# Score buffers of two PSUM banks for a pair of heads, and a fixed order of a pair's products and masks

## The chip, the core and the metric

One program runs on one core of a Trainium2 chip. The metric is the device time of one execution in microseconds (us); of several executions the median is taken. Five engines work side by side: TensorE (PE; PEld is its weight load), VectorE (DVE), ScalarE (ACT), GpSimd (POOL) and SyncE (SP, which here only issues DMAs). TensorE writes its results to PSUM, eight banks of 128 partitions by 512 floats.

## The reference

Block-causal attention (blocks of 64) over 4 batches, 8 heads, 576 positions and 64 channels; then a mixture of 8 experts on the 2304 tokens whose gates are normalised eight times by rows and columns; then a soft mixture of 8 experts with 32 slots.

```python
scores = scale * np.matmul(q, k.transpose(0, 1, 3, 2))
scores = np.where(mask, scores, -1000000000.0)
scores = scores - np.max(scores, axis=-1, keepdims=True)
attn = np.exp(scores)
attn = attn / (np.sum(attn, axis=-1, keepdims=True) + 1e-09)
return np.matmul(attn, v).astype(np.float32)
...
for e in range(E):
    h = np.maximum(x @ w1[e], 0.0)
    ye = h @ w2[e]
    out += P[:, e:e + 1] * ye
```

## The kernel before

Only the attention stage is touched, the first 340 us or so. It works on pairs of heads: 4 batches of 4 pairs. The 576 queries of a head are cut into four tiles of 128 (j = 0 to 3) and a last one of 64; the two heads' last ones share a tile (a = 2, j = 4). A tile of number j needs 128(j+1) keys, so its score product is 128, 256, 384 or 512 columns wide. The list `jobs` has four jobs with j = 0 and 1 only (four steps each, for the first batch, so that the mixture of experts can begin early), four with j = 2, 3 and 4 (five steps) and twelve with all (nine steps). A step is one tile of one head; head 0 and head 1 alternate.

One step `g` of the loop at L598 emits in this order: the scores (`emit_S`; at head 0 for both heads), the row maximum on DVE (`emit_max`), the transposes of the step four before (`emit_T`, on PE, with a copy out of PSUM on ACT, L488), the exponential on ACT (`emit_exp`, L451, with a read of its accumulator), the scaling by the reciprocal sum (`emit_scale`, L457 and L458 on DVE, L471 on POOL), then what `todo` holds: value products (`emit_PV`, L527) and the split of their result into a high and a low part (L545, L549). Then `fill` asks a generator (`moe_stream`) for mixture-of-experts (MoE) matmuls worth a nominal 1200 ns: first layer L174 to L176, second layer L203. It gives none while the batch that it needs next is not through attention.

A planner puts the instructions of each engine into a fixed order ahead of time: by program order among those that are ready in its own forecast, with a tile's slot allocated when one is free. `tc.keep_in_program_order(x)` adds one condition: x comes behind the instruction that was traced just before it on its engine; it doesn't forbid others in between. On the chip each engine takes its instructions in that order and waits on semaphores.

The PSUM banks in the attention stage: two (`m0`, `m1`) for the MoE work and, in the first four jobs, for the transposes; one (`pv`) for the value products; five (`tag="s"`, `SB = 5`) that scores of head 0, scores of head 1 and later transposes take one by one, as they come free. The scores of a pair: two products with 64 rows each (each is two matmul instructions, since it is in float32), head 0 on partitions 0 to 63, head 1 on 64 to 127, in separate banks; then two small bfloat16 products that add the mask. The two halves of TensorE's rows can run at the same time. The last tile (L420 to L426) has eight matmuls into two banks; its transposes (L502 to L509) take two banks, `tp` and `tq`. The probability tiles `pes` (j < 2) and `pe` have three buffers each; a transposed tile frees one.

Loads of MoE weights go through one raw buffer (`r`); L120 (ACT) and L121 (DVE or POOL) split them into a high and a low part, the pieces of the second layer pinned in program order.

Of the kernel before, what the change touches and what calls it, by code (L numbers as in the profile page):

```python
# [7 lines left out]
F32 = mybir.dt.float32  # L8
# [26 lines left out]
def attn_moe_softmoe_kernel(ctx: ExitStack, tc: tile.TileContext, qk1, q, k, v, wg, w1, w2, phi, m2w1, m2w2, cst, out):  # L35
    nc = tc.nc
# [28 lines left out]
    def bank(name):  # L65
        pool, tag = banks[nbank[0] % len(banks)]
        nbank[0] += 1
        return pool.tile([128, 512], F32, tag=tag, name=name)
# [281 lines left out]
    with ExitStack() as actx:  # L350
        ap1 = actx.enter_context(tc.tile_pool(name="at1", bufs=1))
        ap2 = actx.enter_context(tc.tile_pool(name="at2", bufs=2))
        ps = actx.enter_context(tc.tile_pool(name="ps", bufs=1, space=PSUM))

        mask_l = ap1.tile([128, 128], BF16, name="mask_l")
        mask_r = ap1.tile([128, 64], BF16, name="mask_r")
# [5 lines left out]
        def tiles_of(gr):  # L362
            return (G1 if "1" in gr else []) + (G2 if "2" in gr else [])
# [31 lines left out]
            x = qk[n][0][:, 256:S + 64] if gr == "2" else qk[n][0]  # L395
            nc.gpsimd.tensor_scalar(out=x, in0=x, scalar1=0.125, scalar2=1.0, op0=ALU.mult, op1=ALU.mult)

        SB = 5
        EPOOL = False
        PS_ = 3  # L400
        PB_ = 3
# [2 lines left out]
        HD = [slice(0, 64), slice(64, 128)]  # L404

        def emit_S(n, tl):
            a, j = tl
            qt, kt = qk[n]
            if a == 1:
                return st_S[n, j]  # L410
            if a == 0:
                w = 128 * (j + 1)
                ss = [ps.tile([128, 512], F32, tag="s", name="s", bufs=SB) for _ in range(2)]
                for r, s in zip(HD, ss):
                    nc.tensor.matmul(s[:, 0:w], qt[r, 128 * j:128 * j + 128], kt[r, 0, 0:w], start=True, stop=False)  # L415
                for r, s in zip(HD, ss):
                    nc.tensor.matmul(s[:, 128 * j + 64:128 * j + 128], mask_l[r], mask_r[r], start=False, stop=True)
                st_S[n, j] = [ss[1][:, 0:w]]
                return [ss[0][:, 0:w]]
            sv = [ps.tile([128, 512], F32, tag="s", name="sL", bufs=SB)[:, 0:288] for _ in range(2)]  # L420
            for x in range(2):
                for hf in range(2):
                    r = HD[hf]
                    h = hf ^ x
                    nc.tensor.matmul(sv[hf][HD[h]], qt[r, 512 + 64 * x:576 + 64 * x], kt[r, x, 288 * hf:288 * hf + 288], start=True, stop=True)  # L425
            return sv  # L426
# [49 lines left out]
        def emit_T(n, t, pt):  # L476
            p, gr = jobs[n]
            a, j = tiles_of(gr)[t]
            if (a, j) == (0, 0):
                PT[n, 0] = ap1.tile([128, 2, 384], F32, tag="PT0", name="PT0")  # L480
            if (a, j) == (0, 2):
                PT[n, 1] = (ap1.tile([128, 2, 4, 320], F32, tag="PT1", name="PT1"), ap1.tile([64, 2, 64], F32, tag="PT2", name="PT2"))

            def cp(o, i):
                if n < 4 and a == 1:
                    nc.vector.tensor_copy(out=o, in_=i)
                else:
                    nc.scalar.activation(out=o, in_=i, func=AF.Copy)  # L488
            if j < 4:
                if nofill[0]:  # L490
                    tp = bank("tp")
                else:
                    tp = ps.tile([128, 512], F32, tag="s", name="tp", bufs=SB)
                for i in range(j + 1):
                    nc.tensor.transpose(tp[:, 128 * i:128 * i + 128], pt[:, 128 * i:128 * i + 128], ident)  # L495
                if j < 2:
                    cp(PT[n, 0][:, a, 128 * j:128 * j + 128 * (j + 1)], tp[:, 0:128 * (j + 1)])
                else:
                    cp(PT[n, 1][0][:, a, 0:j + 1, 128 * (j - 2):128 * (j - 2) + 128], tp[:, 0:128 * (j + 1)].rearrange("p (i q) -> p i q", q=128))
                return  # L500
            big, small = PT[n, 1]
            tp = ps.tile([128, 512], F32, tag="s", name="tp", bufs=SB)  # L502
            for i in range(4):
                nc.tensor.transpose(tp[:, 128 * i:128 * i + 128], pt[:, 128 * i:128 * i + 128], ident)
            tq = ps.tile([128, 512], F32, tag="s", name="tq", bufs=SB)
            nc.tensor.transpose(tq[0:64, 0:128], pt[:, 512:576], ident)
            for a in range(2):
                cp(big[:, a, :, 256:320], tp.rearrange("p (i a q) -> p a i q", a=2, q=64)[:, a])
            cp(small, tq[0:64, 0:128].rearrange("p (a q) -> p a q", a=2))  # L509
# [88 lines left out]
        for g in range(NG + LT + 6):  # L598
            live = g < NG
            if live:  # L600
                n, t = steps[g]
                p, gr = jobs[n]
                ntl = len(tiles_of(gr))
                tl = tiles_of(gr)[t]
                sv = emit_S(n, tl)
                nm = emit_max(sv)
            fill(FILL * FR)
            if 0 <= g - LT < NG:
                emit_T(*steps[g - LT], st[g - LT][0])
# [46 lines left out]
    tq = [tmp[j // 2][:, H_ * (j % 2):H_ * (j % 2) + H_] for j in range(4)]  # L656
# [245 lines left out]
    for u in range(4, NU - 1):  # L902
        i = ND + u - 4
# [444 lines left out]
```

## Time and profile before

| | before |
|---|---|
| median of 3 runs | 1810.55 us (1809.51 to 1810.71) |
| profiled execution | 1809.36 us |
| its span, first to last instruction | 1807.6 us |
| granted TensorE clock, mean | 0.998 |
| PE, DVE, ACT, POOL busy | 98%, 66%, 32%, 12% of the span |

The page's slices are 45 us each; the attention stage is the first seven and a half. A timeline row merges neighbours of the same kind: start, time from the first one's start to the last one's end, engine, line, operation, what is written and read, shape and count, and in brackets the idle time before it with what ended it. Matmuls overlap, so the distance between two starts says more than a duration.

### The profile page before, as it was taken

The numbers are of one execution on the slowest core, as the hardware profiler recorded it, in microseconds if no ns is written. First come the engines' busy times: TensorE is split into PE (matmuls) and PEld (weight loads), VectorE is DVE, ScalarE is ACT, GpSimd is POOL, SyncE is SP. The second block draws the span as 40 slices with busy tenths as digits, with TensorE's granted clock in tenths as the row PEclk, the third lists the DMA queues.
The fourth block names the chain that finished last, engine by engine and source line by source line (L and its number), as shares of the span: only waits on it lengthen the run. The fifth ranks groups of instructions, "written<-read, shape, count | busy, mean of one in ns | idle before, by whom it ended". The sixth has DMA issues, their size and how long they took to land.

```text
span 1807.6 us, 24545 instructions
## 1 busy us (share of the span) xinstructions
PE 1779.8 (98%) x9239; PEld 1411.1 (78%) x9239; DVE 1197.5 (66%) x2391; ACT 584.7 (32%) x1485; POOL 225.4 (12%) x343
## 2 busy tenths in 40 slices
PE   7999999999999999999999999999999999999997
PEld 4676666787888888888888888888888888888864
DVE  5566555688766676677776666667777766666542
ACT  5666656334322222222222222222222222222232
POOL 4333222033000000000000000000000000000011
PEclk9999999999999999999999999999999999999999
DMA  5432311011000000000000000000000000000877
GB/s 178 128 101 82 101 55 61 13 48 36 24 24 24 24 24 24 24 24 24 17 19 24 24 24 24 24 24 24 24 24 24 24 24 24 24 24 16 298 278 274
DMA packets 79046, 102.98 MB, mean 57 GB/s; under 512 B 4688, under 2 KB 55632, under 8 KB 78928
## 3 DMA queue, kind: packets, MB, share of 16 engines
q1 hardware_dynamic: 78928, 101.42, 16.9%
q8 instruction: 73, 1.20, 0.3%
q14 instruction: 45, 0.37, 0.1%
HBM read 96.68 MB, written 4.72 MB: 56 GB/s over the span
## 4 chain that ended last, share of the span: by engine, by line
PE 91%; DVE 2%; POOL 1%; ACT 1%; issue 1%; DMA 1%; ACTq 0%; POOLq 0%; SPq 0%; DVEq 0%
PE l L203 42%; PE S L804 17%; PE A L804 12%; PE pvp L527 2%; PE tp L495 2%; PE s L415 2%; PE l L854 2%; PE l L853 2%; PE l L852 2%; PE l L174 1%; PE l L176 1%; PE l L175 1%; DMA r<-in_moe_w_dram 1%; PE xt L944 1%; PE sL L425 0%
## 5 line engine op out<-in xcount | busy, mean ns | idle before, releaser
L213 DVE SCALAR_TENSOR_TENSOR acc<-l,P,acc 128x512 f32<-128x512 f32 x504 | 377.9, 750 | 224.3 <-PE l L203 223.8
L203 PE MATMUL l<-w2h,hh 128*128 128x512 f32 x1132 | 447.9, 396 | 1.0 <-ACT hh L807 1.0
L203 PE MATMUL l<-w2h,hl 128*128 128x512 f32 x1132 | 443.0, 391 | 1.3 <-DVE hl L808 1.1
L203 PE MATMUL l<-w2l,hh 128*128 128x512 f32 x1132 | 442.8, 391 | 0.0
L819 DVE TENSOR_TENSOR tmp<-S,tmp 128x512 f32<-128x512 f32 x275 | 185.0, 689 | 138.1 <-PE S L804 136.4
L203 PEld LDWEIGHTS l<-w2h,hl 128*128 128x128 f32 x1132 | 212.9, 188 | 47.7 <-DVE hl L808 1.7
L203 PEld LDWEIGHTS l<-w2h,hh 128*128 128x128 f32 x1132 | 213.2, 188 | 46.1 <-ACT hh L807 1.5
L203 PEld LDWEIGHTS l<-w2l,hh 128*128 128x128 f32 x1132 | 213.3, 188 | 39.9
L807 ACT ACTIVATE hh<-tmp 128x512 fp32r<-128x512 f32 x216 | 136.1, 630 | 290.6 <-DVE tmp L819 261.0
L804 PE MATMUL S<-T,es 128*128 128x512 f32 x660 | 167.3, 389 | 0.0
L778 POOL TENSOR_TENSOR st<-r 128x256 f32<-128x256 f32 x56 | 41.0, 753 | 987.3 <-DMA r<-in_moe_w_dram 987.3
L804 PE MATMUL A<-xh,es 128*128 128x512 f32 x440 | 153.4, 389 | 0.0
L804 PE MATMUL S<-xh,es 128*128 128x512 f32 x440 | 153.4, 389 | 0.0
L808 DVE SCALAR_TENSOR_TENSOR hl<-tmp,hh 128x512 fp32r<-128x512 f32 x216 | 147.9, 685 | 0.8 <-ACT hh L807 0.7
L804 PEld LDWEIGHTS S<-T,es 128*128 128x128 f32 x660 | 123.9, 188 | 25.7
L661 ACT ACTIVATE es<-st 128x256 fp32r<-128x256 f32 x112 | 46.5, 415 | 211.2 <-POOL st L778 112.7
L823 ACT ACTIVATE tmp<-A 128x512 f32<-128x512 f32 x55 | 32.8, 597 | 234.9 <-PE A L804 233.3
L120 ACT ACTIVATE w2h<-r 128x256 fp32r<-128x256 f32 x160 | 54.5, 407 | 144.0 <-PE l L203 126.1
L804 PEld LDWEIGHTS S<-xh,es 128*128 128x128 f32 x440 | 82.6, 188 | 17.1
L804 PEld LDWEIGHTS A<-xh,es 128*128 128x128 f32 x440 | 82.6, 188 | 17.1
L819 DVE TENSOR_TENSOR tmp<-A,tmp 128x512 f32<-128x512 f32 x110 | 75.7, 688 | 16.9 <-PE A L804 16.3
L804 PE MATMUL A<-xl,es 128*128 128x512 f32 x220 | 85.7, 389 | 0.0
(231 smaller groups left out, 2538.5 us busy)
## 6 DMA issues: line engine op xcount, KB each, us to landing
r<-in_moe_w_dram SPq DMA_DIRECT2D x80, 512.0 KB, 3.4
mw<-in_moe_w_dram SPq DMA_DIRECT2D x64, 512.0 KB, 7.4
kraw<-in_k_dram SPq DMA_DIRECT2D x16, 576.0 KB, 3.9
qraw<-in_q_dram SPq DMA_DIRECT2D x16, 320.0 KB, 4.3
v<-in_v_dram SPq DMA_DIRECT2D x16, 256.0 KB, 2.9
out_dram<-ob SPq DMA_DIRECT2D x6, 512.0 KB, 3.5
out_dram<-ob SPq DMA_DIRECT2D x6, 256.0 KB, 2.3
qk<-in_qk_dram SPq DMA_DIRECT2D x4, 256.0 KB, 4.4
```

The lines of the kernel that those rows point to most:

```text
L120: p = [nc.scalar.activation(out=h, in_=r[:, a:a + 256], func=AF.Copy)]
L203: nc.tensor.matmul(o, lh, w[:, kf, :], start=(m == 0), stop=(m == 5))
L213: nc.vector.scalar_tensor_tensor(out=av, in0=o, scalar=P[:, tt, e:e + 1], in1=av, op0=ALU.mult, op1=ALU.add)
L415: nc.tensor.matmul(s[:, 0:w], qt[r, 128 * j:128 * j + 128], kt[r, 0, 0:w], start=True, stop=False)
L495: nc.tensor.transpose(tp[:, 128 * i:128 * i + 128], pt[:, 128 * i:128 * i + 128], ident)
L527: nc.tensor.matmul(o[64 * a:64 * a + 64, lo:hi], w, r(a), start=(m == 0), stop=(m == len(its) - 1))
L661: nc.scalar.activation(out=h, in_=src, func=AF.Copy),
L778: nc.gpsimd.tensor_tensor(out=o, in0=a, in1=b, op=alu)
L804: nc.tensor.matmul(o[:, 0:H_], a[:, k], b[:, k], start=(k == 0 and m == 0), stop=(k == 1 and m == 2))
L807: nc.scalar.activation(out=h, in_=src, func=AF.Relu)
L808: nc.vector.scalar_tensor_tensor(out=lo, in0=src, scalar=0.0, in1=f32(h), op0=ALU.max, op1=ALU.subtract)
L819: nc.vector.tensor_tensor(out=out, in0=o, in1=i, op=ALU.add)
```

## The change

Scores of both heads share one tile of two banks (`s2`), with two such buffers in place of the five single banks; the last tile's scores and the last tile's transposes (`t2`) use the same two buffers; the other transposes get one bank of their own (`tag="tp"`). The second head's product is pinned behind the first head's, and each mask behind what was traced before it. The number of instructions does not change.

```diff
-        SB = 5
...
             if a == 0:
                 w = 128 * (j + 1)
-                ss = [ps.tile([128, 512], F32, tag="s", name="s", bufs=SB) for _ in range(2)]
+                s2 = ps.tile([128, 2, 512], F32, tag="s", name="s", bufs=2)
+                ss = [s2[:, 0], s2[:, 1]]
                 for r, s in zip(HD, ss):
-                    nc.tensor.matmul(s[:, 0:w], qt[r, 128 * j:128 * j + 128], kt[r, 0, 0:w], start=True, stop=False)
+                    i = nc.tensor.matmul(s[:, 0:w], qt[r, 128 * j:128 * j + 128], kt[r, 0, 0:w], start=True, stop=False)
+                    if r is HD[1]:
+                        tc.keep_in_program_order(i)
                 for r, s in zip(HD, ss):
-                    nc.tensor.matmul(s[:, 128 * j + 64:128 * j + 128], mask_l[r], mask_r[r], start=False, stop=True)
+                    tc.keep_in_program_order(nc.tensor.matmul(s[:, 128 * j + 64:128 * j + 128], mask_l[r], mask_r[r], start=False, stop=True))
                 st_S[n, j] = [ss[1][:, 0:w]]
                 return [ss[0][:, 0:w]]
-            sv = [ps.tile([128, 512], F32, tag="s", name="sL", bufs=SB)[:, 0:288] for _ in range(2)]
+            s2 = ps.tile([128, 2, 512], F32, tag="s", name="sL", bufs=2)
+            sv = [s2[:, 0, 0:288], s2[:, 1, 0:288]]
...
                 if nofill[0]:
                     tp = bank("tp")
                 else:
-                    tp = ps.tile([128, 512], F32, tag="s", name="tp", bufs=SB)
+                    tp = ps.tile([128, 512], F32, tag="tp", name="tp")
...
-            tp = ps.tile([128, 512], F32, tag="s", name="tp", bufs=SB)
+            t2 = ps.tile([128, 2, 512], F32, tag="s", name="tp2", bufs=2)
+            tp, tq = t2[:, 0], t2[:, 1]
             for i in range(4):
                 nc.tensor.transpose(tp[:, 128 * i:128 * i + 128], pt[:, 128 * i:128 * i + 128], ident)
-            tq = ps.tile([128, 512], F32, tag="s", name="tq", bufs=SB)
             nc.tensor.transpose(tq[0:64, 0:128], pt[:, 512:576], ident)
```

## Rows read from the trace of the kernel before

**Rows 1.** The page: busy time (us, share, instructions) and shares of the last chain.
```profile
PE 1779.8 (98%) x9239; PEld 1411.1 (78%) x9239; DVE 1197.5 (66%) x2391; ACT 584.7 (32%) x1485; POOL 225.4 (12%) x343
...
PE 91%; DVE 2%; POOL 1%; ACT 1%; issue 1%; DMA 1%; ACTq 0%; POOLq 0%; SPq 0%; DVEq 0%
```

**Rows 2.** Timeline of PE, 195 to 210 us, a nine-step job with fill.
```profile
202.79 0.70 PE L415 MATMUL s<-kraw,qraw 64*128 64x256 f32 x4
...
207.37 0.92 PE L415 MATMUL s<-kraw,qraw 64*128 64x384 f32 x4
...
208.51 2.42 PE L527 MATMUL pvp<-PT,v 128*64 128x320 f32 x20
```

**Rows 3.** Timeline of PE, 225.9 to 228 us, a pair that comes apart.
```profile
225.99 0.70 PE L415 MATMUL s<-kraw,qraw 64*128 64x256 f32 x2
226.62 0.50 PE L203 MATMUL l<-w2h,hl 128*128 128x512 f32 x1
...
227.71 0.66 PE L495 MATMUL tp<-ident,pe 128*128 128x128 f32 x4
```

**Rows 4.** Timeline of PE at 184.8 us, masks that stand apart.
```profile
184.83 0.20 PE L417 MATMUL s<-mask_r,mask_l 64*128 64x64 bf16 x2
```

**Rows 5.** Timeline of PE, 147 to 157 us, a crowded pass.
```profile
147.34 0.63 PE L495 MATMUL tp<-ident,pe 128*128 128x128 f32 x4
147.89 0.91 PE L415 MATMUL s<-kraw,qraw 64*128 64x256 f32 x4
...
149.72 0.48 PE L203 MATMUL l<-w2h,hl 128*128 128x512 f32 x1
150.13 1.19 PE L415 MATMUL s<-kraw,qraw 64*128 64x384 f32 x4
...
151.28 0.33 PE L495 MATMUL tp<-ident,pes 128*128 128x128 f32 x1
...
155.83 1.03 PE L425 MATMUL sL<-kraw,qraw 64*64 64x288 f32 x8
```

**Rows 6.** Timeline of ACT, 147 to 152 us, the same pass.
```profile
147.57 0.49 ACT L488 ACTIVATE PT<-tp 128x384 f32<-128x384 f32 x1
...
150.78 0.27 ACT L488 ACTIVATE PT<-tq 64x128 f32<-64x128 f32 x1
151.65 0.47 ACT L451 ACTIVATE pes<-s,nm 128x256 f32<-128x256 f32 x1 [0.60 <-PE tp L495]
```

**Rows 7.** Timeline of PE, 4 to 21 us, the start.
```profile
4.47 1.21 PE L415 MATMUL s<-qk 64*128 64x256 f32 x4
...
6.59 1.47 PE L415 MATMUL s<-qk 64*128 64x256 f32 x4
...
16.27 1.22 PE L415 MATMUL s<-qk 64*128 64x256 f32 x2
...
19.71 0.79 PE L415 MATMUL s<-qk 64*128 64x256 f32 x1
...
20.91 1.11 PE L495 MATMUL tp<-ident,pes 128*128 128x128 f32 x4
```

**Rows 8.** Timeline of ACT, 12 to 13.4 us, the start.
```profile
12.00 1.03 ACT L120 ACTIVATE w1h<-r 128x256 fp32r<-128x256 f32 x3 [5.21 <-DMA r<-in_moe_w_dram]
12.93 0.45 ACT L451 ACTIVATE pes<-s,nm 128x256 f32<-128x256 f32 x1
```

**Rows 9.** Timeline of PE, 61 to 73 us, a five-step job and the next.
```profile
61.05 0.72 PE L425 MATMUL sL<-kraw,qraw 64*64 64x288 f32 x8
...
72.10 1.09 PE L495 MATMUL tp<-ident,pe 128*128 128x128 f32 x4 [3.11 <-ACT pe L451]
```

**Rows 10.** Timeline of ACT, 63 to 72 us, the same jobs.
```profile
63.47 0.67 ACT L451 ACTIVATE pe<-s,nm 128x512 f32<-128x512 f32 x1
...
70.45 1.03 ACT L120 ACTIVATE w2h<-r 128x256 fp32r<-128x256 f32 x3 [3.81 <-DMA r<-in_moe_w_dram]
```

**Rows 11.** Windows: stretch, its length, busy time (and instructions) of PE, PEld, DVE, ACT, POOL, clock, DMA share, GB/s.
```profile
72.10:75.50 3.40, 3.40 (x10) 2.54 (x10) 2.10 (x7) 2.35 (x8) 2.07 (x3) 0.52 0.00 0
```

## Prediction

> **What bounds the kernel now.** I read the page's busy table first, then the chain that ended last: TensorE (PE) carries 91% of the chain and is busy for 98% of the span [rows 1]. PE time saved or lost in the attention stage (until 340 us) therefore moves the end by as much, unless a wait takes it back. Nothing after that stage is touched. A busy PE is not a working PE, though: matmuls are recorded as busy while they wait for a bank. So I read the timeline of PE by what one group of score products takes in a crowded place and in a free one, and looked up what each waited for in the timeline of ScalarE (ACT).
>
> The stage has three faces. (a) A start of some 35 us without mixture-of-experts (MoE) work to fill gaps. (b) Long stretches where MoE matmuls fill PE: there a whole pair of 256 or 384 columns takes 0.70 and 0.92 us [rows 2]. (c) Four crowded passes of a nine-step job (near 90, 150, 163 and 250 us) with hardly any fill, where the same pairs take 0.91 and 1.19 us [rows 5], because the second head's product finds no free bank.
>
> **The change, part by part.** Before, five single banks serve scores and transposes alike. After, scores have two buffers of two banks each, transposes one bank, and only the last tile's transposes (L502 to L507) take a score buffer. No instruction is added or removed, so the sum is made of waits and order alone.
>
> *Pairs that come apart are joined.* At 226 us one head went first, a MoE matmul of 0.50 came between, the other followed: 1.72 us from 225.99 to the transposes at 227.71 [rows 3], against 0.70 for a whole pair [rows 2]. Less the MoE matmul's share that is 0.5 to 0.8; I take -0.7, once.
>
> *The late second head.* In the crowded passes a 256-column pair takes 0.91 in place of 0.70 [rows 2, 5], four times. A last-tile product group takes 1.03 there [rows 5] and 0.72 in a free place [rows 9], three times. With both banks free at once this goes: -4 x 0.21 - 3 x 0.31 = -1.8. Bounds: none of it (the pair waits as a whole and PE has nothing else) to all; I take all, since by the order of allocation the buffer these two need was left one or more steps earlier.
>
> *The pair that must now wait.* In a nine-step job the 384-column pair gets the buffer of the 256-column pair just before it (the last tile's transposes sit in the other one). It cannot start before that pair's second exponential is done. In the crowded pass it starts at 150.13, and that exponential runs at 151.65, itself released by a transpose [rows 6], the one at 151.28 [rows 5]. So the pair goes behind the 20 value products that follow. Where fill is at hand this is a swap and costs nothing: at 207.37 the pair stands directly ahead of 2.42 us of value products [rows 2], and its own transposes come four steps later. In the crowded pass the value products wait for the last copy of the transposes, at 150.78 for 0.27 [rows 6]; between the single MoE matmul at 149.72 and 151.28 [rows 5] PE has only this pair to do. Its 0.92 moves out of a hole into a full stretch: 4 x 0.92 = +3.7. Bounds: 0, if a transpose that the single bank holds back falls into that hole, to 4 x 1.19 = +4.8.
>
> *One bank for transposes.* Each step's transposes now wait for the copy of the step before. Mostly that copy is long done; in one step of each nine-step job it isn't: transposes began at 147.34 while ACT copied the previous ones from 147.57 for 0.49 [rows 5, 6], so they would move by some 0.7. The 256-column pair queued next, at 147.89, can take their place, and elsewhere MoE matmuls can. Cost 0; without that cover 12 x 0.7 = 8.4, which needs every such step to stand bare, and eight of the twelve passes have fill. Queued behind a waiting transpose on PE is everything; the next exponential waits for transposes too, because the probability tiles have three buffers.
>
> *The start.* Here the banks of the transposes are others and stay, so five score banks become two pairs. Two pairs came apart: first head 1.22 at 16.27, second head 1.20 (19.71 to 20.91), against 1.21 for a whole one; that is 1.2 each, -2.4. But the fourth pair ran at 6.59 in time that was idle anyway [rows 7]; it now waits for the exponential at 12.93, behind weight splits on ACT that wait for a DMA [rows 8], and its 1.2 falls into the full stretch: +1.2. Net -1.2; bounds -2.4 (still hidden) and +1.2 (the joined pairs wait as long as they save).
>
> *The pins.* They give an order (second head behind first, masks behind both), no adjacency. Three pairs have six MoE matmuls between products and masks, as the masks at 184.83 [rows 4]; a mask pair lasts 0.20, so joining them is worth at most 0.6. I take 0.
>
> **Sum.** -0.7 - 1.8 + 3.7 + 0 - 1.2 + 0 = 0.0 us. The profiled execution took 1809.36 us (span 1807.6 and 1.8 around it) and would stay there; the median of the runs, 1810.55, is 1.2 above it, so the forecast for the median is 1810.5.
>
> A rule of the skill speaks for a gain here. The page TensorEngine Tiling (Array Packing) of the Trainium skill, section Key Properties, says that a change of tiling mode drains TensorE. By it every group that stands apart pays one more drain on the way in and out, the three mask groups too, and if the pins joined those as well the sum would be -0.6 in place of 0.0, 1809.9. The trace agrees in sign, with 0.5 to 0.8 at the pair that came apart [rows 3], but shows no drain apart from a wait.
>
> **The rivals.** *Faster.* The crowded passes lose nothing: the planner lays held-back transposes or MoE matmuls into the hole at 150, the +3.7 falls away. 1810.5 - 3.7 = 1806.8, and 1805.6 with the start at its better end. For it: the six MoE matmuls of those passes are movable. Against: their order comes from a planner that doesn't know when a DMA lands. A neighbour: the 3.1 us hole before 72.10 [rows 9] may close by reordering alone, another -4.7 (next rival), to about 1801.
>
> *Slower.* One more such hole. In five-step jobs the last tile's products start at 61.05 [rows 9], but the buffer that they will need is freed by the exponential at 63.47 for 0.67 [rows 10]; so they move by 3 us, and their exponentials and copies with them, towards ACT's weight splits, which stood 3.81 us for a DMA at 70.45 [rows 10]. The point from which it decides: the MoE matmuls at hand run out before ACT resumes. Price, from the one hole that is there: 3.11 us idle [rows 9], then a granted clock of 0.52, near the lower of its two levels (1.2 GHz), for 3.4 us [rows 11], in which half of the time is lost: 3.1 + 1.6 = 4.7. The time would be 1815.2. For it: three five-step jobs have the products 2 to 3 us ahead of that exponential. Against: the wait is on weights, whatever the scores do, and later products are also work that could fill the hole. The page TensorE: Matmul & The Clock Gate of the Trainium skill, section HAM oscillation, says that long idle gaps throttle the clock again and that this is paid at each gap; the trace agrees, with 0.52 after that gap, and by the rule alone without a new gap nothing is lost.
>
> *It doesn't do what it says.* Splits remain, since pins don't forbid MoE matmuls in between and the banks were seldom the cause: the gains of 0.7 and 1.8 stay out and, with fewer joined pairs, the waits too. About 1810 to 1812; this is no change.
>
> **How the numbers follow.** Runs of this kernel differ by 1.2 us, and 0.2% (3.6 us) is about what can be told from no change: 1806.9 to 1814.2 counts as the same. The forecast and the last rival together get 0.41 (0.31 and 0.10), the faster rival 0.33, the slower 0.26. Many small terms of both signs and a whole stage reordered make the tails wide. The lower end takes the crowded passes at 0, the start at -2.4 and about half of a closed hole: 1802. The upper end takes the passes at +4.8, the start at +1.2 and most of a new hole: 1817.5. The likeliest case alone spans 1807 to 1814.
>
> **What would show it.** Right: both heads' products start within 10 ns of each other in all 64 pairs; the 384-column pair follows the value products in every nine-step job; the 256-column pair takes 0.70 in the crowded passes; last-tile products 0.72 everywhere; the crowded job still takes about 13 us; the span up to the end of attention moves by less than 3 us. Wrong: a new idle gap of PE over 2 us, or the one before 72.10 gone; crowded jobs longer or shorter by over 0.5 us each; attention's end moved by over 4 us.

## The result, and the profile after

The kernel after takes 1821.58 us (median of six runs, 1817.97 to 1823.5) against 1810.03 for the kernel before beside it: a ratio of 1.006 with an interval of 1.0046 to 1.0075, slower by 11.5 us where no change was forecast.

The page of the kernel after, busy times and shares of the chain that ended last, answers to [rows 1]:

```profile
PE 1783.5 (98%) x9239; PEld 1406.7 (77%) x9239; DVE 1192.8 (66%) x2391; ACT 586.9 (32%) x1485; POOL 225.2 (12%) x343
...
PE 92%; DVE 2%; POOL 1%; DMA 1%; ACT 1%; issue 1%; ACTq 0%; POOLq 0%; SPq 0%; DVEq 0%
```

With the same instructions PE is busy 3.7 us longer. A wait of one head's product doesn't show as idle time of PE here, because the other half of the array is still at work meanwhile; so where the time went is read from the attention stage in three stretches, cut at the starts of score pairs that exist in every kernel: the start up to the third five-step job (36 MoE matmuls done by then in every kernel here), the third and fourth five-step job (96 more), and the twelve nine-step jobs up to the start of the last value product (554 or 555 more, with 36 small ones of the gates; one is worth 0.2). Times in us, worked out from the starts in the PE timeline; kernels e1 to e12 are the experiments below:

| kernel | start, to | two five-step jobs | nine-step jobs | end of attention |
|---|---|---|---|---|
| before | 51.40 | 34.30 | 255.99 | 341.69 |
| after | 51.41 | 34.06 | 265.35 | 350.82 |
| e9, after without pins (same order) | 54.41 | 32.86 | 265.90 | 353.17 |
| e1, pins alone | 57.77 | 30.77 | 256.98 | 345.52 |
| e2, one transpose bank | 58.17 | 31.00 | 266.52 | 355.69 |
| e3, two transpose banks | 52.62 | 34.78 | 259.74 | 347.14 |
| e4, last tile out too | 53.44 | 29.50 | 257.21 | 340.15 |
| e5, cut in mid pair | 52.00 | 31.27 | 263.04 | 346.31 |
| e6, cut between pairs | 51.99 | 30.61 | 257.20 | 339.80 |
| e7, e4 and pairs pinned | 54.10 | 29.62 | 254.38 | 338.10 |
| e8, five banks, pinned | 49.35 | 30.96 | 256.17 | 336.48 |
| e10 | 49.30 | 29.50 | 254.16 | 332.96 |
| e11 | 49.39 | 29.51 | 254.19 | 333.09 |
| e12 | 48.38 | 29.51 | 254.32 | 332.21 |

In these two executions the attention stage ends 9.1 us later, and all of it lies in the nine-step jobs: +9.4, of which the crowded passes have most (the one from 148.35 to 164.13 took 15.8 us; its like before, 145.05 to 158.07, 13.0, with four MoE matmuls, 0.9 us, less in it). From the end of attention on, both kernels are alike (1467.7 and 1467.2 us). The profiled execution of after is its fastest of six, so 9.1 is less than the 11.5 of the medians; the last section shows that its start met a better clock.

The timeline of PE in that crowded pass of the kernel after (start, time to the last end, engine, line, operation, count) answers to [rows 5]; L415 and L419 are a pair's products and masks, L498 the transposes, L530 the value products, L428 the last tile:

```profile
149.71 0.70 PE L415 MATMUL s<-kraw,qraw 64*128 64x256 f32 x2
150.33 0.66 PE L498 MATMUL tp<-ident,pe 128*128 128x128 f32 x4
150.92 0.48 PE L415 MATMUL s<-kraw,qraw 64*128 64x256 f32 x1
150.93 0.20 PE L419 MATMUL s<-mask_r,mask_l 64*128 64x64 bf16 x1
151.24 0.38 PE L415 MATMUL s<-kraw,qraw 64*128 64x256 f32 x1
...
153.81 0.75 PE L530 MATMUL pvp<-PT,v 128*64 128x320 f32 x2
154.49 0.92 PE L415 MATMUL s<-kraw,qraw 64*128 64x384 f32 x4
...
155.37 0.49 PE L530 MATMUL pvp<-PT,v 128*64 128x320 f32 x2
...
159.43 0.70 PE L428 MATMUL sL<-kraw,qraw 64*64 64x288 f32 x2
160.06 0.43 PE L498 MATMUL tp<-ident,pes 128*128 128x128 f32 x2
160.42 0.71 PE L428 MATMUL sL<-kraw,qraw 64*64 64x288 f32 x6
161.06 0.65 PE L530 MATMUL pvp<-PT,v 128*64 128x256 f32 x2
161.64 0.55 PE L498 MATMUL tp<-ident,pe 128*128 128x128 f32 x3
162.11 0.86 PE L530 MATMUL pvp<-PT,v 128*64 128x256 f32 x6
```

Before, each of these four groups stood whole: four products of a pair in one row at 147.89, eight last-tile products at 155.83 [rows 5], and the value products in one row each, by PE's timeline of the kernel before:

```profile
151.54 2.42 PE L527 MATMUL pvp<-PT,v 128*64 128x320 f32 x20
...
157.27 0.87 PE L527 MATMUL pvp<-PT,v 128*64 128x256 f32 x8
```

Now each is cut once, that is, other work stands inside it. The cut always falls after the first instructions of one head, so that the two halves of the array, which could run at the same time, run one after the other: the first head's product from 149.71 to the transposes at 150.33 takes 0.62, then the second head starts alone. In the nine-step jobs of after eighteen groups are cut so: five last-tile groups and three of 256-column value products (by transposes), five 256-column pairs (three by transposes, two by MoE matmuls), and five of 320-column value products (by a 384-column pair). Before, it was one, a pair cut by a MoE matmul [rows 3]; it is one of the two in after as well. Pairs whose masks alone stand apart are not counted.

When the cutters become free is read from ACT's timeline of the kernel after, in the same pass:

```profile
149.24 0.49 ACT L491 ACTIVATE PT<-tp 128x384 f32<-128x384 f32 x1
...
153.79 0.46 ACT L454 ACTIVATE pes<-s,nm 128x256 f32<-128x256 f32 x1
```

The copy at 149.24 empties the single transpose bank at 149.73, just after the first head's product has started at 149.71. PE's order is fixed ahead of time, so it is the planner, in a forecast that is not on record, that put the first head's product first, then the transposes, which were traced earlier, then the second head; what the chip did fits such a forecast, and e3 below tests it. The exponential at 153.79 is the second one of the 256-column pair; with the read of its accumulator it ends at 154.35 and frees the buffer of the 384-column pair, which then, at 154.49, stands in the middle of value products that had already begun.

The groups of instructions by line, nine-step jobs alone (from the first score pair to 362 us), busy time and mean ns of one, for the kernel before:

```profile
L527 PE MATMUL pvp<-PT,v 128*64 128x320 f32 (+4 forms) x356 | 42.2, 368 | 0.0
L415 PE MATMUL s<-kraw,qraw 64*128 64x128 f32 (+3 forms) x192 | 41.9, 482 | 0.0
...
L425 PE MATMUL sL<-kraw,qraw 64*64 64x288 f32 x96 | 9.5, 428 | 0.0
```

for the kernel after:

```profile
L530 PE MATMUL pvp<-PT,v 128*64 128x320 f32 (+4 forms) x356 | 47.7, 369 | 0.0
L415 PE MATMUL s<-kraw,qraw 64*128 64x128 f32 (+3 forms) x192 | 42.3, 482 | 0.0
...
L428 PE MATMUL sL<-kraw,qraw 64*64 64x288 f32 x96 | 12.0, 428 | 0.0
```

and for e3, where the transposes have two banks again:

```profile
L530 PE MATMUL pvp<-PT,v 128*64 128x320 f32 (+4 forms) x356 | 45.8, 368 | 0.0
L415 PE MATMUL s<-kraw,qraw 64*128 64x128 f32 (+3 forms) x192 | 39.6, 482 | 0.1
...
L428 PE MATMUL sL<-kraw,qraw 64*64 64x288 f32 x96 | 8.6, 428 | 0.0
```

The mean of one instruction is the same throughout, so no wait hides inside a matmul's own record, as the prediction had it; the busy time of a line, which counts overlapped time once, is not the same. Value products: 42.2 to 47.7. Last-tile products: 9.5 to 12.0, and 8.6 where nothing cuts them. Scores: 41.9 to 42.3, since the late second heads are gone (39.6 in e3) and the cuts took that back.

### The profile page after: what moved, and what is told of

Its sections match the earlier page's. It is cut to its first block, busy times and chain, and to the rows that moved or that the text cites. A ratio compares the mean times of both kernels' runs of the same rounds, so it can differ in the third digit from the quotient of the medians.

```text
span 1816.2 us, 24540 instructions
## 1 busy us (share of the span) xinstructions
PE 1783.5 (98%) x9239; PEld 1406.7 (77%) x9239; DVE 1192.8 (66%) x2391; ACT 586.9 (32%) x1485; POOL 225.2 (12%) x343
## 4 chain that ended last, share of the span: by engine, by line
PE 92%; DVE 2%; POOL 1%; DMA 1%; ACT 1%; issue 1%; ACTq 0%; POOLq 0%; SPq 0%; DVEq 0%
PE l L203 42%; PE S L807 16%; PE A L807 12%; PE pvp L530 3%; PE tp L498 2%; PE s L415 2%; PE l L174 2%; PE l L857 1%; PE l L856 1%; PE l L855 1%; PE l L176 1%; PE l L175 1%; DMA r<-in_moe_w_dram 1%; PE sL L428 1%; PE xt L947 0%
```

## The experiments

**Theory.** The loss is cuts: a group of two heads' products loses the overlap of its halves wherever a step of other work stands inside it. The cuts by transposes come from the single transpose bank, those of the 320-column value products from the pair that waits for its buffer. **Rivals.** The pair buffers alone make the loss; the pins do; or the cuts are only a sign of waits elsewhere.

**e1, the pins alone**, on the kernel before:

```diff
-                    nc.tensor.matmul(s[:, 0:w], qt[r, ...
+                    i = nc.tensor.matmul(s[:, 0:w], qt[r, ...
+                    if r is HD[1]:
+                        tc.keep_in_program_order(i)
...
-                    nc.tensor.matmul(s[:, 128 * j + 64:128 * j + 128], ...
+                    tc.keep_in_program_order(nc.tensor.matmul(s[:, 128 * j + 64:128 * j + 128], ...
```

> Kernel before, with the pins alone (second head's product and both masks kept in program order), five single banks as before. Theory (time goes where a group of two heads' products is cut apart by other work on PE): in the order of PE's instructions five more groups are cut than before (a 128- and a 384-column pair by four transposes, two groups of 256-column value products by a score product, one start pair by more), at 0.55 to 0.66 each +2 to +3 us, 1812 to 1813. Rival (the pins are harmless or join groups): 1809.4 to 1810.

Measured 1813.0 against 1809.18, ratio 1.0028 (1.0017 to 1.0039). Slower, as its theory expected, not harmless. But its order has nine cut groups against five in the kernel before, and all that are new lie ahead of the nine-step jobs; these have the same one cut as before and took 1.0 more. In its profile the start took 6.4 more, half of it given back behind it, and the clock rose 7.1 us later there (last section). So that the cuts make the 3.8 us is not shown.

**e2, the single transpose bank alone**, without pair buffers or pins:

```diff
-        SB = 5
+        SB = 4
...
-                    tp = ps.tile([128, 512], F32, tag="s", name="tp", bufs=SB)
+                    tp = ps.tile([128, 512], F32, tag="tp", name="tp")
```

> Kernel before, but the transposes of the first four tiles have one bank of their own and four single banks are left for scores; no pair buffers, no pins. Theory A (the single transpose bank lets transposes become free one group at a time, and they land inside groups of last-tile products, 256-column value products and 256-column score pairs): the order of PE shows 32 groups cut against 9, some 20 of the dear kind at 0.55 to 0.66, +11 to +13 us, 1821 to 1823. Rival B (the pair buffers make the loss, through the pair that waits for an exponential): within 1 us of before, 1809 to 1811.

Measured 1822.9, ratio 1.0071 (1.0056 to 1.0087): the whole loss without any pair buffer, and 10.5 us of it in the nine-step jobs. The rival that blames the pair buffers alone falls. But the eight banks are all taken, so the bank for the transposes costs the scores one of their five, and this is a second difference. Of the 15 groups cut in its nine-step jobs six are cut by transposes alone; four are 320-column value products cut by 384-column pairs and two are such pairs cut in turn, here without any pair buffer. This run therefore doesn't separate the single transpose bank from the shortage of score banks; e3 does.

**e3, pair buffers and pins, but two banks for transposes**, which they share with the value products:

```diff
-                    tp = ps.tile([128, 512], F32, tag="tp", name="tp")
+                    tp = ps.tile([128, 512], F32, tag="pv", name="tp", bufs=2)
...
-            o = ps.tile([128, 512], F32, tag="pv", name="pvp")
+            o = ps.tile([128, 512], F32, tag="pv", name="pvp", bufs=2)
```

> Kernel after, with one edit: transposes and value products share two banks in place of one bank each. Theory A: the cuts by transposes go (five last-tile groups, four 256-column value groups, three 256-column score pairs: 12 x about 0.57 = 6.8), the cuts of the 320-column value products by the waiting 384-column pair stay (six x 0.66 = 4.0): 1821.6 - 6.8 = 1814.8. Rival B (all of the loss is the pair buffers'): 1820 to 1822. Rival C (the transposes are all of it): about 1809.

Measured 1813.37, ratio 1.0024 (1.0015 to 1.0032). All cuts by transposes in the nine-step jobs are gone, the five by the 384-column pair are still there, and these jobs take 259.74 in place of 265.35 (265.9 in e9): -5.6 to -6.2, where 6.8 was expected. What remains, +3.8 over the kernel before, is not the five cuts alone (5 x 0.68 = 3.4), since the late second heads, 3.2 by the lines above, should have paid for those. The windows of the nine-step jobs (length, then busy time and count of PE, PEld, DVE, ACT, POOL, clock, DMA share, GB/s) tell where they went; before, after, e3 and e12, each from its own run:

```profile
85.70:341.69 255.99, 255.27 (x1611) 170.76 (x1610) 149.01 (x491) 154.30 (x501) 70.18 (x121) 1.00 0.22 72
```
```profile
85.47:350.82 265.35, 264.64 (x1612) 171.22 (x1611) 144.37 (x491) 156.41 (x501) 70.28 (x121) 1.00 0.22 69
```
```profile
87.40:347.14 259.74, 256.42 (x1612) 169.11 (x1611) 144.40 (x491) 155.93 (x501) 70.46 (x121) 1.00 0.22 71
```
```profile
77.89:332.21 254.32, 252.49 (x1611) 167.37 (x1611) 144.89 (x491) 154.97 (x501) 69.78 (x121) 1.00 0.22 72
```

PE idles 259.74 - 256.42 = 3.3 us in e3, 0.7 before and after, 1.8 in e12. Once the pairs are quick, crowded passes wait for exponentials and transposes: the gain comes, and a wait takes most of it.

**e4, the last tile's transposes out of the pair buffers**, into the two shared banks:

```diff
-            t2 = ps.tile([128, 2, 512], F32, tag="s", name="tp2", bufs=2)
-            tp, tq = t2[:, 0], t2[:, 1]
+            tp, tq = [ps.tile([128, 512], F32, tag="pv", name=x, bufs=2) for x in ("tp", "tq")]
```

> As the kernel with two shared banks for transposes and value products, and the last tile's transposes moved out of the pair buffers into those two banks as single-bank tiles, so that a 384-column pair finds the buffer of the 128-column pair free. Theory A with the second cause: the six cuts of 320-column value products go as well, -4.0 against the kernel with shared banks alone: 1809 to 1811, at or below the kernel before. Rival (the 384-column pair's wait was not what cut the value products, or the last tile's transposes now wait for the value products' copies instead): 1814 to 1817.

Measured 1806.78, ratio 0.9983 (0.9972 to 0.9994), below the kernel before. In the nine-step jobs no value products are cut any more. Two 384-column pairs are, by the transpose into `tq` (1.71 in place of 0.88 each), so the nine-step jobs gain 2.5 of the expected 4.0; the five-step jobs gain 5.3 on e3, on which more below.

**e5 and e6, cuts made on purpose** in the kernel before. In the step of the 320-column value products the step's transposes stand inside the group (15 of 16), after the fifth product, between the two heads of one step (e5, the `5` below), or after the fourth, between two steps (e6, a `4` there). In both, these transposes and value products are also kept in program order:

```diff
+                    if g == 1 and 2 * m + a == 5 and defer:
+                        defer.pop()()
...
-                emit_T(*steps[g - LT], st[g - LT][0])
+                if g in pv1:
+                    defer.append(lambda g=g: emit_T(*steps[g - LT], st[g - LT][0], True))
+                else:
+                    emit_T(*steps[g - LT], st[g - LT][0])
```

> Kernel before, with one thing moved: in the step of each job's 320-column value products the transposes of that step stand after the fifth of the ten value products, in the middle of one step's two heads, in place of ahead of the first (15 of the 16 groups are cut so; nothing else is cut or added). Theory A (a cut between the two heads costs two changes of mode and the overlap of the halves): +0.66 each, as the cut groups took 3.03 in place of 2.37 in the kernel after: 15 x 0.66 = +9.9, 1819 to 1820. Rival (a group that is cut is only a sign of a wait elsewhere, the cut itself is cheap): 1809 to 1811.

> The same with the transposes after the fourth value product, between two steps, where both heads of a step stay together. Theory A: only the changes of mode are paid, 0.2 to 0.3 each by the first matmul of a group: 15 x 0.25 = +3 to +4.5, 1812.5 to 1814. Rival (the changes of mode are the whole price, the overlap of heads none of it): as much as with the cut in the middle of a pair.

Measured 1816.49 with the cut in the middle of a pair, ratio 1.0048 (1.0035 to 1.006), and 1809.6 with the cut between pairs, 1.0008 (0.9999 to 1.0017). The same group in both, PE's timeline of e5 and then of e6:

```profile
208.65 1.83 PE L533 MATMUL pvp<-PT,v 128*64 128x320 f32 x10
210.41 0.33 PE L495 MATMUL tp<-ident,pes 128*128 128x128 f32 x1
210.66 1.34 PE L533 MATMUL pvp<-PT,v 128*64 128x320 f32 x10
211.94 0.50 PE L203 MATMUL l<-w2h,hh 128*128 128x512 f32 x1
```
```profile
205.50 1.30 PE L533 MATMUL pvp<-PT,v 128*64 128x320 f32 x8
206.73 0.33 PE L495 MATMUL tp<-ident,pes 128*128 128x128 f32 x1
206.98 1.35 PE L533 MATMUL pvp<-PT,v 128*64 128x320 f32 x12
208.26 0.50 PE L203 MATMUL l<-w2h,hh 128*128 128x512 f32 x1
```

From start to start the two parts take 1.76 + 1.28 = 3.04 in e5 and 1.23 + 1.28 = 2.51 in e6; a whole group takes 2.35 (142.49 to 144.84 in e12, below). So a cut between the heads costs 0.69, the same cut two instructions earlier 0.16. Both have the same changes of mode; the difference, 0.53, is the overlap of the halves. What is left for the changes of mode is 0.16 at most, less than the 0.2 to 0.3 that was expected of e6. Over the whole kernel the two runs differ by 6.9 us in the medians, 0.46 for each of the 15 groups. This settles the rival "only a sign": the cut itself costs. e5 stayed 2.3 us short of the +9.9 that its theory gave; why is not shown.

The page TensorEngine Tiling (Array Packing) of the Trainium skill, section Key Properties, has both parts: different tiles can work in parallel, and a change of mode drains TensorE. The trace agrees with the first, and puts it at 0.53 here; for the second it leaves 0.16 at most.

**e7, e4 with the first head's product pinned too**; and **e8, the five single banks of before** with score products, masks and value products pinned:

```diff
-                    if r is HD[1]:
-                        tc.keep_in_program_order(i)
+                    tc.keep_in_program_order(i)
```

and, in e8 only,

```diff
-                    nc.tensor.matmul(o[64 * a:64 * a + 64, lo:hi], w, r(a), ...
+                    i_ = nc.tensor.matmul(o[64 * a:64 * a + 64, lo:hi], w, r(a), ...
+                    tc.keep_in_program_order(i_)
```

> Pair buffers, two banks shared by transposes and value products, the last tile's transposes in those, and one more pin: the first head's product too is kept in program order, so that the pair as a whole can't start ahead of work that is traced before it. In the order of PE one group of the start stays cut (against 8 without that pin). Theory A: the two 384-column pairs cut by a transpose (1.71 in place of 0.88) and the 256-column pair cut by a MoE matmul (1.28 in place of 0.66) are whole, -2.3, and the start's pair -1.0: about 1803 to 1805 against 1806.8. Rival (held-back pairs make PE or ScalarE wait): 1808 to 1812.

> Kernel before with its five single banks, all score products, masks and value products kept in program order: no group is cut in the order of PE at all, but pairs still wait for their second bank. Theory A: the start's cut groups and the pair of 226 us are worth about -2.5, the late heads stay: 1806 to 1809. Rival (program order makes value products and pairs wait for transposes and exponentials): 1811 to 1816.

Measured 1805.11 (0.997, 0.9958 to 0.9981) and 1804.04 (0.9975, 0.9964 to 0.9986). Both beat the kernel before. A pin on the second head alone lets the first go early and leaves room behind it; a pin on the first head holds the whole pair behind earlier work. With it the three cuts that e4 has in its nine-step jobs are gone, and these take 2.8 less; the intervals of e4 and e7 overlap. e8 needs no other bank and has no cut at all. Its nine-step jobs stay at 256.2, late second heads and all; its profile is shorter by 2.1 in the start and 3.3 in the two five-step jobs, but in that of the kernel before the clock rose later in the start and fell in a five-step job (last section), so how much of its 4.9 us is the pins' is open.

**e9, the kernel after without its pins:**

> Kernel after without its pins (second head's products and the masks free again), pair buffers and single transpose bank kept. The order of the instructions on all five engines comes out the same as that of the kernel after. Theory A (the banks alone cut the groups): as the kernel after, 1820 to 1823. Rival (the pins act through waits that the order doesn't show): more than 2 us off that.

Measured 1821.91, ratio 1.0071 (1.0058 to 1.0084). Beside the pair buffers the pins change nothing: the order on PE, ACT, DVE and POOL is the same instruction by instruction, and the banks make it.

**e10 to e12, for a version that beats both.** e10 is e7 with the value products pinned as in e8 and the last-tile products in the same way; e11 adds the edit below; e12 has this edit on e7:

```diff
+                if (n, j) == (1, 0):
+                    ss = [ps.tile([128, 512], F32, tag="pv", name="s", bufs=2) for _ in range(2)]
+                else:
```

> The layout with two banks shared by transposes and value products and the last tile's transposes in them, with score products, masks, last-tile products and value products all in program order: no group cut at all. Theory A: against the run in which only score products and masks were pinned (1805.1) one group at the start less is cut: 1803 to 1806. Rival (pinned groups wait for what is traced ahead of them): 1807 to 1810.

> The same, and at the start the third pair of scores takes the two shared banks, which stand empty then, so that three pairs in place of two can be ready before the first exponential, as with five single banks nearly. Theory: the start up to the same MoE work took some 3 us more with two pairs than with five single banks (54.1 against 49.4 to the same 36 MoE matmuls); half of that comes back, part of it swallowed by the later wait for weights: 1801 to 1804. Rival (the start is bound by the loads and by exponentials, not by banks): as without, 1803 to 1806.

> The third pair in the shared banks, with only score products and masks pinned (value and last-tile products free). Theory: as the run before it within 1.5 us, 1801 to 1804, as only one last-tile group more is cut; rival (the pins on value products cost waits at the start): 2 us or more below the fully pinned one.

Measured 1803.74, 1802.81 and 1802.18, ratios 0.9968 (0.9956 to 0.998), 0.9965 (0.9952 to 0.9977) and 0.9964 (0.995 to 0.9978): 0.3 to 0.4% below the kernel before. The three can't be told apart, so the third pair is not shown to be worth anything. The crowded pass of e12 on PE, whole groups throughout:

```profile
139.19 0.70 PE L418 MATMUL s<-kraw,qraw 64*128 64x256 f32 x4
...
141.28 0.92 PE L418 MATMUL s<-kraw,qraw 64*128 64x384 f32 x4
...
142.49 2.42 PE L531 MATMUL pvp<-PT,v 128*64 128x320 f32 x20
144.84 0.33 PE L500 MATMUL tp<-ident,pes 128*128 128x128 f32 x1
...
147.01 0.72 PE L430 MATMUL sL<-kraw,qraw 64*64 64x288 f32 x8
...
148.13 0.87 PE L531 MATMUL pvp<-PT,v 128*64 128x256 f32 x8
```

## Why the prediction was wrong, point by point

**One bank for transposes, cost 0: the step that failed.** The wait was seen rightly (transposes behind the copy of the step before, by some 0.7), and so was that other work would take their place. The error was to call that free. The work that takes the place is half a group, and the transposes then stand in its middle. Three 256-column pairs (1.28 in place of 0.66), five last-tile groups (1.27 in place of 0.65) and three groups of value products (1.37 in place of 0.80), start to start in the timeline of after against e3, are 1.9 + 3.1 + 1.7 = 6.7. So the term put at 0 measured about 6.7 by the rows, and a second bank took back 5.6 to 6.2 (e3).

**The pair that must now wait, +3.7.** The cause held: the 384-column pair starts at 154.49, after the second exponential of the 256-column pair. But it did not go behind the value products, it went into them: 3.03 in place of 2.35, five times 0.68 = 3.4. That the size came out near is luck, since the pair's own 0.92 did not move into a full stretch; it cost the value products their overlap. In the other seven nine-step jobs it stands ahead of them as before, a swap at no cost as forecast.

**The late second head, -1.8.** The lines say more: 3.2 (2.3 on scores, 0.9 on last-tile products, e3 against before), because two 128-column and four 384-column pairs had a late second head too. All thirteen are gone in after. But where no cuts by transposes take that time, PE's idle time does: it took 2.6 back in e3 and 1.1 in e12. The bounds, from none to all, were the right ones; to take all was not.

**Pairs that come apart, -0.7, and the pins, 0.** The pair of 226 us comes apart again, now at 232.67, 1.72 us as before; pinned order is not adjacency, as the prediction itself said of the masks. The gain stayed out, and another such pair came at 182.49. In the kernel after the pins are worth 0, as forecast (e9).

**The start, -1.2.** The two pairs that came apart are whole in after, as forecast, but up to the nine-step jobs five other groups are cut, against four before. The start took 51.41 against 51.40, but the clock rose at 18.99 us in after and at 30.98 before (last section). In e9, the same order, it rose at 29.59, near that of before, and the start took 54.41. So at a like clock the start is 3.0 longer, not 1.2 shorter, outside the bound of +1.2; 1.4 of it is given back in the two five-step jobs.

**The slower rival**, a new hole in the five-step jobs, is not what happened, though its time of 1815.2 lay on the right side. The hole that there was shrank from 3.11 [rows 9] to 2.41, by PE's timeline of after:

```profile
72.23 0.63 PE L498 MATMUL tp<-ident,pe 128*128 128x128 f32 x4 [2.41 <-POOL w2l L121]
```

Behind it the granted clock fell as before (a mean of 0.70 from 72 to 76 us); in e9 a hole of 2.42 at 73.20 left it at 1.00.

Sum for the nine-step jobs: 6.7 + 3.4 + 0.6 (the new 256-column pair cut by MoE matmuls) - 3.2 = +7.5, against +9.4 measured (+9.9 in e9). About 1 more lies in the six fuller jobs, 0.0 to 0.4 each; the rest is not settled. The end of attention moves by 9.1 in the profiled execution and by 11.5, as the medians do, in e9, whose order is the same and whose start is 3.0 longer.

The forecast therefore fell on one sentence, not on the range of a price: "the 256-column pair queued next can take their place". Its own bound without that cover was 8.4, near what came in size, though it meant bare waits and not cuts, and it was left out of the range because eight of twelve passes have fill. It was mostly the few passes without fill that paid, and they pay in cuts. The range itself has a slip: the terms named for its lower end give 1810.5 - 3.7 - 1.2 - 2.4 = 1803.2, not 1802.

**The faster rival's neighbour came true elsewhere.** In the five kernels with the last tile's transposes out of the pair buffers (e4, e7, e10 to e12) the two five-step jobs take 29.5 to 29.6, whatever the start before them; in the others 30.6 to 34.8. ACT's timeline of after, then of e12, in the fourth five-step job:

```profile
70.07 0.72 ACT L120 ACTIVATE w2h<-r 128x256 fp32r<-128x256 f32 x2 [3.07 <-DMA r<-in_moe_w_dram]
70.70 0.48 ACT L454 ACTIVATE pe<-sL,nm 128x288 f32<-128x288 f32 x1
```
```profile
64.65 0.50 ACT L456 ACTIVATE pe<-sL,nm 128x288 f32<-128x288 f32 x1 [1.02 <-PE tp L500]
...
67.39 0.42 ACT L120 ACTIVATE w2h<-r 128x256 fp32r<-128x256 f32 x1 [0.99 <-DMA r<-in_moe_w_dram]
```

In after the last tile's exponential stands behind a weight split that waits for its load; in e12 ahead of it, and PE has no gap. The windows 66 to 78 us of before and of e12:

```profile
66.00:78.00 12.00, 8.89 (x47) 6.37 (x47) 6.38 (x14) 4.99 (x17) 2.80 (x4) 0.86 0.30 96
```
```profile
66.00:78.00 12.00, 12.00 (x88) 8.49 (x87) 7.40 (x24) 7.35 (x24) 4.04 (x6) 1.00 0.25 90
```

The job falls from 19.55 to 14.75 us (66.15 to 85.70 before, 63.14 to 77.89 in e12), 4.8, the 4.7 that the prediction set on this hole. The granted clock stays at 1.00 without it. Here the page TensorE: Matmul & The Clock Gate of the Trainium skill, section HAM oscillation, fits: without the idle gap there is no slow stretch behind it to pay. Not all of the 4.8 is the order's: in e1 and e8 the exponential stands behind the split as well, yet the hole is 1.08 and 1.27, the clock does not fall, and the job takes 16.0 and 16.2.

## What to carry to other kernels

Two products that share the array by halves are best treated as one unit of work: what came between them here cost their overlap (0.53 of 0.69 us), so before banks are dealt out anew, look at what each new wait will let into the middle of such a group. Where a planner orders the work, hold the first instruction of a group, not only the second; a pin on the second lets others in between. Putting a transposing step that had several banks to run ahead in on one bank was not free here, even though each wait was covered by other work.

## What the hardware showed beside it

At the start, matmuls take up to twice as long for a while, and that while differs between executions of the same order. Transposes on PE's timeline in after, then in e9, whose order is the same, at 0.33 and at 0.47 for one:

```profile
19.62 0.33 PE L498 MATMUL tp<-ident,pes 128*128 128x128 f32 x1
...
22.95 0.67 PE L498 MATMUL tp<-ident,pes 128*128 128x128 f32 x3 [0.32 <-POOL pes L474]
```
```profile
19.94 0.47 PE L496 MATMUL tp<-ident,pes 128*128 128x128 f32 x1
...
24.24 0.90 PE L496 MATMUL tp<-ident,pes 128*128 128x128 f32 x3
```

The last slow transpose lies at 18.7 us in after, 28.2 in e9, 29.9 before, and between 18.7 and 35.8 in all the kernels here. Four slow ones take 1.11 at 20.91 [rows 7], as long as the 1.09 at 72.10 [rows 9], where the granted clock is 0.52 [rows 11], and 0.63 elsewhere [rows 5]. So the start runs at or near the lower of the two levels (1.2 GHz). The column of the granted clock reads 1.00 there, but that is no reading: the trace's own records of the clock begin with a rise to the upper level (2.4 GHz), at 18.99 us in after, 29.59 in e9 and 30.98 before, in each kernel 0.2 to 2.3 us behind its last slow transpose, and the time ahead of the first record is counted as full speed.

When the clock rises differs by 10.6 us between two executions of one order, and the start with it: 51.41 in after, 54.41 in e9, part of it given back at the wait for weights behind. Starts can therefore be compared only where the clock rose at a like time. It rose at 38.07 in e1, 34.99 in e7, 26.66 in e8 and 20.44 to 23.03 in e10 to e12, so the starts of these kernels, short or long, don't show what their banks and pins are worth there. Neither does the expectation of e11, which set the start of e7 against that of e8.

The clock fell again in the fourth five-step job in three profiles alone, those of before, after and e3, behind holes of 3.11, 2.41 and 1.96 us, and these three have the longest pairs of five-step jobs (34.06 to 34.78). Behind the end of attention it fell once more in e3 to e6 and e12, where two idle gaps of about 1 us stand close together, but not in the other nine, which have the same two gaps.
